# Shorter fill matmuls, a last product in two parts, and another planned order in a one-core attention and mixer kernel on Trainium2

## The chip, the cores and the metric

The kernel runs on one core of a Trainium2 chip. The core has a matmul engine (TensorE, PE in the profile, with its weight loads as PEld), three engines for elementwise work and copies (VectorE or DVE, ScalarE or ACT, GpSimd or POOL), SyncE (SP), which here only issues transfers, and 16 DMA engines fed by queues. Each engine works through its own instructions in the order in which the program gives them and waits at semaphores for the others. PE multiplies a stationary operand (at most 128 x 128, loaded into the array) by a moving one and adds into banks of PSUM, each 128 partitions x 512 f32. The metric is the time of one execution on the device in microseconds (us), lower is better; the median of several runs is given.

## The reference

Attention over a window of 128 keys with a linear bias by distance, 8 batches, 8 heads, 576 positions, 64 numbers per head, and then a mixer: a hidden layer over the tokens and one over the channels, each with a residual. Inputs and outputs are f32.

```python
scores = q @ k.transpose(0, 1, 3, 2) / 8.0
bias = slopes[h] * -abs(i - j);  mask = (i - j >= 0) & (i - j < 128)
attn = softmax(where(mask, scores + bias, -1e9))
x = (attn @ v).transpose(0, 2, 1, 3).reshape(8, 576, 512)
h = relu(x.transpose(0, 2, 1) @ w_tok1) @ w_tok2      # w_tok1 576x256, w_tok2 256x576
u = x + h.transpose(0, 2, 1)
out = u + relu(u @ w_ch1) @ w_ch2                     # w_ch1 512x1536, w_ch2 1536x512
```

## The kernel before

All matmuls are in bf16. A batch of 576 positions is four blocks of 128 and a tail of 64; two batches form a pair, and the two tails of a pair share one block of 128. For every batch there are two strands of work. The `side` strand brings the attention and the token half: loads of q, k, v by POOL with a cast to bf16 on the way (`load`, L515), transposes of q and k, on PE for the first ten blocks (L630, copied out on L636) and by DMA from SP for later ones (L619), scores (L670, with the bias on L679), exp on ACT (L693), the mask on DVE (L703), the product with v (L736), reciprocal and normalising on DVE (L749, L752), then the two token products (L781 and L791; relu on L799 or L800; L820 and L824) and the sum u in `ub` (L842). u is transposed to `uT` by DMA (L850, four transfers a batch) or by PE (L859, L865). The `main` strand is the channel half: the first product in chunks of four matmuls with 512 columns (`chunk`, L1021; L1006 in the head of the kernel), relu on ACT or DVE (L1027, L1028), sums of the hidden blocks (L1046), the tail's share (L1064, L1069, L1109, L1116, stored on L1126), and `second`: the second product, 512 x 1536 by 1536 x 512, as seven products of half size in the manner of Strassen (`PRODUCTS`, numbered 1 to 7). Each product is twelve matmuls of 256 columns (L1198, two groups of six) into a bank, where later products add to what is there. When a product is done, DVE adds it to u or to an output tile `ob` (`evict`, L1169), and the last addition to a tile is followed by a store of 256 KB (L1181), by SP, or by POOL in batches 5 and 6. In the last batch, part of the first channel product is done by seven products too (`unit`, L943, with keeps on L958 and L959 and joins on L967).

The weight pieces of w_ch1 (`A0` to `A3`) and w_ch2 (`B0` to `B3`) and those of the token layer come in on POOL's queue among the loads of the first pair, in the order of the string `LOADS`: `k7` is the k of the seventh block, and so on. POOL issues them one after another, each as soon as its buffer is free.

The order of the whole work is not that of the program text. Each operation is entered into `Plan` with an engine, a modelled cost, a rank, and the buffers that it makes and uses. `Plan.run` (from L118) replays the kernel by its costs: at each step the engine that can start first takes the ready operation of the lowest rank; the rank is the place of the operation in its strand, shifted by a random number of up to 1500 either way (`SEEDS`, one seed per part; part 0 is the first `side`, part b + 1 holds `main` of batch b and `side` of batch b + 1; a seed of 0 means no shift). `emit` (L301) then writes the instructions in the order of the replayed times. What stands where, on every engine, therefore hangs on the modelled costs and on the seeds; the chip keeps to this order on each engine and takes its own times.

Where the replay sees PE wait in the first 60 us, `emit` puts matmuls on a tile of zeros into a bank that is free then (`spin`, L1250, the matmul on L1254), so that PE doesn't stand still. A fill is made for each wait over 60 ns (250 after 20 us). Its length in columns is the wait, plus 150 ns, times 1.2 for waits before 7.4 us; after that it is the wait times 2.4, less 60 ns if it lies after 20 us. There are 43 such matmuls, of 19196 columns together.

At the end of the kernel, the last batch's products come in the order 1, 5, 6, 2, 3, 7, 4. Between products 7 and 4, nine matmuls of the tail (L1109) have their place. The last three transfers are a store of product 7's tile, two small ones of the tail (64 KB each) and then the 256 KB store behind product 4.

Of the kernel before, what the change touches and what calls it, by code (L numbers as in the profile page):

```python
# [11 lines left out]
ALU = mybir.AluOpType  # L12
# [53 lines left out]
class Plan:  # L66
# [51 lines left out]
    def run(self):  # L118
# [87 lines left out]
        while todo:  # L206
            best = None
            for e, c in cand.items():
                pick, early = None, None
                for o in c:  # L210
                    if e == "POOL" and o is not pool[sent]:
                        continue
                    t = max(ready[o], free[e])
# [46 lines left out]
            if e == "PE":  # L260
                slow = 2.0 if t < WARM else 1.0
                if t > free[e] + 1.0:
                    self.gaps.append((free[e], t))
                    if t > free[e] + 3000:
                        slow = 1.6
                    t += 60.0
                elif o.mode != mode:
                    t += 95.0
                mode = o.mode
                o.t0 = t  # L270
                free[e] = t + o.cost * slow
                o.done = free[e] + 165.0
            elif e == "ACT":
                o.t0, free[e], o.done = t, t + o.cost - 115, t + o.cost
            elif e == "DVE":
                o.t0, free[e], o.done = t, t + max(o.cost - 80, 50), t + o.cost
            elif e == "SP":
                o.t0 = t
                if o.bus:
                    free[e] = t + 1310.0  # L280
                    if o.bus > 1500 and len(turns) > 1:
                        free[e] = max(free[e], turns[-2].done + 1100)
                    turns.append(o)
                    send(o, t + 300, 1, TURN[o.bus > 1500][0], TURN[o.bus > 1500][1])
                else:
                    free[e] = t + 590
                    send(o, t + 300, 1, STORE, 1010.0)
            else:
                o.t0 = t
                free[e] = t + o.cost  # L290
                send(o, t + o.cost, 0, STORE if o.packets < 0 else o.packets * PACKET, 1010.0 if o.packets < 0 else LATE[t > FETCH])
                lanes.append(o)
                sent += 1
# [7 lines left out]
    def emit(self, spin):  # L301
        banks = self.rings["ps"]
        fills = []
        for a, z in self.gaps:
            if a < FILL and z - a > (250 if a > DENSE else 60):
                for i, log in enumerate(banks.log):
                    spans = [(min(u.t0 for u in b.users), max(u.done for u in b.users)) for b in log]
                    if all(z1 < a - 50 or a1 >= z for a1, z1 in spans):
                        fills.append((a, i, (z - a + MORE) * 1.2 if a < CHILLY else (z - a - (60 if a > DENSE else 0)) * 2.4))
                        break  # L310
        work = [(o.t0, o.n, o.emit) for o in self.ops]
        work += [(a, -1, lambda i=i, n=n: spin(banks.slots[i], n)) for a, i, n in fills]
        for _, _, go in sorted(work, key=lambda w: w[:2]):
            go()
# [19 lines left out]
RANKH = 0  # L334
RELU = 350
SUMS_AT = 60e3
SEEDS = [45795, 495947, 190309, 331881, 0, 67117, 67408, 179769, 445757]
SHIFT = 1500.0
UNIT_LATE = False
SECOND_LATE = True  # L340
# [8 lines left out]
FILL = 60000.0  # L349
DENSE = 20000.0  # L350
CHILLY = 7400.0
MORE = 150.0
START = 2700.0
PACKET = 0.813
LATE = (2400.0, 2790.0)
# [5 lines left out]
EARLY = 1  # L361


LOADS = ("k3 q3 q2 k2 k1 q1 v0 W2 k8 q8 v2 v1 v3 v8 W1 q7 k7 A0 k5 q5 k4 v5 "
         "q4 A1 v4 k6 q6 A2 v7 v6 A3 T0 B0 B1 B2 B3")


# [1 line left out]
def kernel(  # L369
# [50 lines left out]
    def bank(choice=ONE):  # L420
        return plan.buf("ps", choice)
# [289 lines left out]
    def values(pr, blk, half, pb, rank):  # L711
# [12 lines left out]
        for es in ([[0, 1]] if both else [[0], [1]]):  # L724
# [7 lines left out]
            for at, e in enumerate(es):  # L732
                def go(e=e, at=at, view=view):
                    mms = [(a, z, kind, vb, i, h) for a, z, kind, vb in work for i, h in enumerate(HEADS[e])]
                    for m, (a, z, kind, vb, i, h) in enumerate(mms):
                        pe_.matmul(view()[a:z, at, i, :], lhsT=pb()[:, e, i, kind, a:z], rhs=vb()[:, h, 0 : D + 1],  # L736
                                   start=m == 0, stop=m == len(mms) - 1, skip_group_check=True)

                rk = rank(240)
                plan.op("PE", 120 * len(work) + (110 if tail and half is None else 0), go, rk,  # L740
                        mode=2 if half is not None else 0, reads=[(pb, e)], uses=[w[3] for w in work],
                        **({"adds": ot} if at else {"makes": ot}))

# [391 lines left out]
    def second(b, rank, r2, ss, sums, ub):  # L1135
        pr, half = b // 2, b % 2
        g1, g2, g3 = bank(ANY), bank(ANY), bank(ANY)
        obs = {}
        capt = {}

        def s_of(i):
            return lambda t, c: ss()[:, "124".index(i), t, c * P : (c + 1) * P]
# [44 lines left out]
                plan.op("SP", 550, store, rk, uses=[ob])  # L1187

        DONE = {1: (0, 0, False), 5: (1, 1, False), 6: (0, 1, False), 7: (1, 1, True), 2: (0, 0, True), 3: (0, 1, True), 4: (1, 0, True)}
        for m in PRODUCTS:  # L1190
            l, w, s, tt = L[m]
            bk = BANK[m]
            for g in range(2):
# [18 lines left out]
                if m in AFTER:  # L1212
                    needs.append(capt[AFTER[m]])
                op = plan.op("PE", 656, go, rank(656), reads=rd, needs=needs,
                             **({"makes": bk} if g == 0 and m not in AFTER else {"adds": bk}))
                if SECOND_LATE and g == 0 and m not in AFTER:
                    marks["wait"].append(op)
            evict(m, bk, *DONE[m])

    def along(base, length, total):  # L1220
        done = [0.0]
# [68 lines left out]
```

## Time and profile before

| what | value |
| --- | --- |
| median of 3 runs | 279.54 us (279.27 to 280.08) |
| the profiled execution | 280.54 us |
| its span in the profile | 278.6 us |
| mean granted clock of TensorE | 0.997 |
| PE busy | 271.4 us, 97% of the span |
| DVE, ACT, POOL busy | 208.0, 136.0, 116.0 us |
| moved by DMA | 38.43 MB, mean 138 GB/s |

The span is the time between the first and the last record of the profile; the execution's own time is 1.94 us longer. Times in views count from the start of the span. Matmuls are pipelined: the duration of a record (379 ns for 512 columns) is longer than its distance to the next one, so PE's busy time joins overlapping records, and a short wait can be hidden in it. The waits view has one row for each pair of a waiting line and what it waited for, with the sum in us, the number of waits and the longest. The chain of work is followed back from the last instruction, and its pieces are given with start, length and line. A view by stretches gives the length of each stretch and then, engine by engine, its busy time and the number of instructions.

### The profile page before, as it was taken

The numbers are of one execution on the slowest core, as the hardware profiler recorded it, in microseconds if no ns is written. First come the engines' busy times: TensorE is split into PE (matmuls) and PEld (weight loads), VectorE is DVE, ScalarE is ACT, GpSimd is POOL, SyncE is SP. The second block draws the span as 40 slices with busy tenths as digits, with TensorE's granted clock in tenths as the row PEclk, the third lists the DMA queues.
The fourth block names the chain that finished last, engine by engine and source line by source line (L and its number), as shares of the span: only waits on it lengthen the run. The fifth ranks groups of instructions, "written<-read, shape, count | busy, mean of one in ns | idle before, by whom it ended". The sixth has DMA issues, their size and how long they took to land.

```text
span 278.6 us, 6964 instructions
## 1 busy us (share of the span) xinstructions
PE 271.4 (97%) x2825; PEld 180.0 (65%) x2825; DVE 208.0 (75%) x485; ACT 136.0 (49%) x219; POOL 116.0 (42%) x146
## 2 busy tenths in 40 slices
PE   7999999999999999999999999999999999999994
PEld 3664765675686556585567655486667645689883
DVE  7566689978897559862989479673989549876982
ACT  5561885336960189206961097206870079205610
POOL 8999765940256027900486009700472220013000
PEclk9999999999999999999999999999999999999998
DMA  9999999999899999999999979999499750043014
GB/s 133 155 138 152 182 190 192 155 125 203 141 113 100 172 251 123 123 142 180 182 133 158 205 191 88 148 138 240 69 115 99 197 142 2 2 118 129 0 53 137
DMA packets 167535, 38.43 MB, mean 138 GB/s; under 512 B 155792, under 2 KB 166672, under 8 KB 167504
## 3 DMA queue, kind: packets, MB, share of 16 engines
q0 software_dynamic: 116112, 20.03, 92.8%
q1 hardware_dynamic: 50352, 17.70, 32.9%
q8 instruction: 22, 0.36, 0.6%
q10 hardware_dynamic: 1040, 0.26, 0.4%
q14 instruction: 9, 0.07, 0.1%
HBM read 35.85 MB, written 9.44 MB: 163 GB/s over the span
## 4 chain that ended last, share of the span: by engine, by line
PE 85%; DMA 6%; POOL 3%; DVE 2%; issue 1%; ACT 1%; SPq 0%; POOLq 0%
PE ps L1198 25%; PE ps L1021 25%; PE ps L736 6%; PE ps L670 5%; PE ps L824 5%; PE ps L781 5%; PE ps L1064 4%; PE ps L943 3%; PE ps L1109 3%; POOL qk L515 3%; DMA qk<-in_k_dram 2%; DMA qk<-in_q_dram 2%; DMA uT<-ub 1%; PE ps L630 1%; PE ps L791 1%
## 5 line engine op out<-in xcount | busy, mean ns | idle before, releaser
L1021 PE MATMUL ps<-uT,WC 128*128 128x512 bf16 x328 | 79.3, 379 | 0.8 <-DMA uT<-ub 0.7
L693 ACT ACTIVATE pe<-ps 128x1024 bf16<-128x1024 f32 (+1 forms) x76 | 63.4, 888 | 30.4 <-PE ps L670 30.1
L515 POOL DMA_DIRECT2D v<-in_v_dram x40 | 34.0, 860 | 92.8 <-PE ps L736 89.0
L1027 ACT ACTIVATE r<-ps 128x512 bf16<-128x512 f32 x75 | 44.4, 601 | 41.4 <-PE ps L1021 39.6
L1021 PEld LDWEIGHTS <-WC 128*128 128x128 bf16 x328 | 29.1, 98 | 31.1 <-issue 2.3
L703 DVE TENSOR_TENSOR pe<-pe,mask 128x1024 bf16<-128x1024 bf16 (+1 forms) x64 | 38.1, 608 | 9.0 <-ACT pe L693 8.5
L1198 PEld LDWEIGHTS <-r 128*128 128x128 bf16 x384 | 37.1, 98 | 7.3 <-issue 0.2
L515 POOL DMA_DIRECT2D qk<-in_k_dram x39 | 33.8, 873 | 2.9 <-DMA v<-in_v_dram 1.4
L515 POOL DMA_DIRECT2D qk<-in_q_dram x39 | 33.5, 864 | 2.4 <-DMA WC<-in_moe_w_ch_dram 1.3
L1198 PEld LDWEIGHTS <-s 128*128 128x128 bf16 x288 | 27.5, 98 | 5.9 <-issue 1.3
L752 DVE TENSOR_TENSOR xb<-ps,rt 128x256 bf16<-128x256 f32 (+1 forms) x72 | 29.0, 416 | 0.7
L736 PEld LDWEIGHTS <-pe 128*128 128x128 bf16 (+1 forms) x560 | 22.4, 100 | 9.2 <-DVE pe L703 2.1
L736 PE MATMUL ps<-v,pe 128*128 128x65 bf16 (+1 forms) x560 | 26.5, 194 | 0.1
L1198 PE MATMUL ps<-WC,r 128*128 128x256 bf16 x192 | 25.4, 273 | 0.0
L1198 PE MATMUL ps<-WT,s 128*128 128x256 bf16 x192 | 24.6, 273 | 0.0
L1198 PE MATMUL ps<-WT,r 128*128 128x256 bf16 x192 | 23.9, 273 | 0.0
L1169 DVE TENSOR_TENSOR ob<-ps,ub 128x512 f32<-128x512 f32 x22 | 15.0, 685 | 10.3 <-PE ps L1198 10.1
L842 DVE TENSOR_TENSOR ub<-ps,xb 128x512 bf16<-128x512 f32 x34 | 21.2, 681 | 1.9 <-PE ps L824 1.8
L670 PEld LDWEIGHTS <-qkT 64*128 64x128 bf16 x560 | 14.8, 94 | 11.2 <-issue 9.8
L670 PE MATMUL ps<-qkT 64*128 64x128 bf16 (+1 forms) x304 | 19.4, 216 | 0.0
L749 DVE RECIPROCAL rt<-ps 128x4 f32<-128x4 f32 (+1 forms) x76 | 12.4, 175 | 8.8 <-PE ps L736 8.2
L1069 ACT ACTIVATE r2t<-ps 128x512 bf16<-128x512 f32 x12 | 7.2, 602 | 22.5 <-PE ps L1064 22.5
(95 smaller groups left out, 340.1 us busy)
## 6 DMA issues: line engine op xcount, KB each, us to landing
out_dram<-ob SPq DMA_DIRECT2D x17, 256.0 KB, 2.6
v<-in_v_dram POOLq DMA_DIRECT2D x32, 128.0 KB, 5.3
qk<-in_k_dram POOLq DMA_DIRECT2D x31, 128.0 KB, 5.5
qk<-in_q_dram POOLq DMA_DIRECT2D x31, 128.0 KB, 5.0
WC<-in_moe_w_ch_dram POOLq DMA_DIRECT2D x8, 384.0 KB, 9.1
out_dram<-raw SPq DMA_DIRECT2D x7, 256.0 KB, 2.8
out_dram<-ob POOLq DMA_DIRECT2D x5, 256.0 KB, 3.4
out_dram<-raw POOLq DMA_DIRECT2D x3, 256.0 KB, 2.9
```

The lines of the kernel that those rows point to most:

```text
L515: nc.gpsimd.dma_start(out=to()[p0 : p0 + n, :, :], in_=rows(src, b, s0, n))
L670: pe_.matmul(wide(e)[:, i, kind, a:z], lhsT=ts[kb]()[e * D : (e + 1) * D, NHP + i, :], rhs=ts[blk]()[e * D : (e + 1) * D, i, a:z], start=n ...
L693: act_.activation(out=pb()[:, e, :, lo:, c0:c1_], in_=wide(e)[:, :, lo:, c0:c1_], func=ACT.Exp, scale=scale)
L703: dve_.tensor_tensor(out=o, in0=o, in1=heads(mk, es), op=ALU.mult)
L736: pe_.matmul(view()[a:z, at, i, :], lhsT=pb()[:, e, i, kind, a:z], rhs=vb()[:, h, 0 : D + 1], start=m == 0, stop=m == len(mms) - 1, skip_g ...
L752: dve_.tensor_tensor(out=x4(), in0=view()[r0:r1_, :, :, 0:D], in1=rt()[r0:r1_, 0:n, :, :].broadcast_to([r1_ - r0, n, 4, D]), op=ALU.mult)
L781: pe_.matmul(t1[j]()[:, :], lhsT=W1[:, c, j * P : (j + 1) * P], rhs=xb()[:, blk, :], start=c == 0, stop=False)
L842: plan.op("DVE", 690, lambda blk=blk, ht=ht, hs=hs: dve_.tensor_tensor(out=ub()[:, blk, :], in0=ht()[:, hs], in1=xb()[:, blk, :], op=ALU.a ...
L1021: pe_.matmul(ct()[:, :], lhsT=WC1[:, cb, t * P : (t + 1) * P], rhs=uT()[:, cb, :], start=cb == 0, stop=cb == NCB - 1)
L1027: plan.op("ACT", 600, lambda t=t, ct=ct: act_.activation(out=r2()[:, t, :], in_=ct()[:, :], func=ACT.Relu), rk, part=(r2, t), uses=[ct], o ...
L1169: dve_.tensor_tensor(out=v, in0=bk().rearrange("p (c n) -> p c n", c=2), in1=src, op=ALU.add)
L1198: pe_.matmul(bk()[:, c * HN : (c + 1) * HN], lhsT=l(t, c), rhs=w(t), start=first, stop=g == 1 and t == HK - 1, skip_group_check=True)
```

## The change

1. Fills: a wait is filled if it is over 60 ns before 7.4 us, over 170 ns from there to 20 us and over 250 ns after that; the 150 ns are no longer added, and after 7.4 us the fill is shorter by 120 ns. There are 37 matmuls of 16296 columns.
2. Loads: `k2` and `q2` swap places, and so the order `q7 k7 A0 k5 q5 k4` becomes `q7 q5 k7 A0 k5 k4`.
3. Planner: a store's modelled transfer goes by its cost (half for a half store), a matmul of the product with v is put at 123 ns instead of 120, and five seeds are others. From the second batch on the order of operations is a different one; the operations are the same.
4. The last batch: product 2 moves to the end, in two parts (`last_product`). Each part is six matmuls into a bank of its own, an addition on DVE of 128 x 256 with what product 1 left in `ob`, and a store of 128 KB, the first by SP and the second by ACT. The first part stands behind product 7 and the second behind product 4. The nine matmuls of the tail that stood between 7 and 4 come earlier.

In the instructions as they are written out, the matmuls apart from the fills and last_product are the same in number and shape, and so are the changes from one kind of matmul to another. In the head, the fill of two matmuls that stood between the transposes of q7, k7 and the six of L824 now stands ahead of the transposes (two of 348 columns).

```diff
-                    send(o, t + 300, 1, STORE, 1010.0)
+                    send(o, t + 300, 1, STORE * o.cost / 550, 1010.0)
...
-            if a < FILL and z - a > (250 if a > DENSE else 60):
+            if a < FILL and z - a > (250 if a > DENSE else 60 if a < CHILLY else 170):
...
-                        fills.append((a, i, (z - a + MORE) * 1.2 if a < CHILLY else (z - a - (60 if a > DENSE else 0)) * 2.4))
+                        fills.append((a, i, (z - a) * 1.2 if a < CHILLY else (z - a - 120) * 2.4))
...
-SEEDS = [45795, 495947, 190309, 331881, 0, 67117, 67408, 179769, 445757]
+SEEDS = [45795, 495947, 190309, 317838, 0, 119438, 0, 583887, 0]
...
-LOADS = ("k3 q3 q2 k2 k1 q1 v0 W2 k8 q8 v2 v1 v3 v8 W1 q7 k7 A0 k5 q5 k4 v5 "
+LOADS = ("k3 q3 k2 q2 k1 q1 v0 W2 k8 q8 v2 v1 v3 v8 W1 q7 q5 k7 A0 k5 k4 v5 "
...
-                plan.op("PE", 120 * len(work) + (110 if tail and half is None else 0), go, rk,
+                plan.op("PE", 123 * len(work) + (110 if tail and half is None else 0), go, rk,
...
-        for m in PRODUCTS:
+        for m in PRODUCTS if b < B - 1 else [x for x in PRODUCTS if x != 2] + [2]:
+            if b == B - 1 and m == 2:
+                last_product(b, rank, r2, obs[0, 0], [opened[7], op])
+                continue
...
+    def last_product(b, rank, r2, old, last):
+        for c in range(2):
+            bk, ob = bank(ANY), plan.buf("ob")
+            def go(c=c, bk=bk):
+                for t in range(HK):
+                    pe_.matmul(bk()[:, 0:HN], lhsT=r2()[:, HK + t, c * P : (c + 1) * P], rhs=WC2[:, HK + t, 0:HN],
+                               start=t == 0, stop=t == HK - 1)
+            def add(c=c, bk=bk, ob=ob):
+                dve_.tensor_tensor(out=ob()[:, 0:HN], in0=bk()[:, 0:HN], in1=old()[:, c * HN : (c + 1) * HN], op=ALU.add)
+            def store(c=c, ob=ob):
+                (nc.sync, nc.scalar)[c].dma_start(out=out[b, c * P : (c + 1) * P, 0:HN], in_=ob()[:, 0:HN])
+            rk = rank(656)
+            plan.op("PE", 656, go, rk, reads=[(r2, HK + t) for t in range(HK)], needs=lc2[HK : 2 * HK], makes=bk,
+                    behind=last[c : c + 1])
+            plan.op("DVE", 425, add, rk, makes=ob, uses=[bk, old])
+            plan.op("SP", 275, store, rk, uses=[ob])
```

More of the change, by code (lines that the diff above doesn't have):

```diff
@@ L351 @@
 CHILLY = 7400.0
-MORE = 150.0
 START = 2700.0
@@ L1138, in second @@
         obs = {}
-        capt = {}
+        capt, opened = {}, {}
         def s_of(i):
```

1 line of the change is left out of this document (added).

## The prediction

> **What bounds the kernel now.** I read the page's first three sections, then TensorE's own waits, then its busy time by stretch, and only then the places where a wait stands.
>
> ```profile
> PE 271.4 (97%) x2825; PEld 180.0 (65%) x2825; DVE 208.0 (75%) x485; ACT 136.0 (49%) x219; POOL 116.0 (42%) x146
> ...
> PEclk9999999999999999999999999999999999999998
> ...
> PE 85%; DMA 6%; POOL 3%; DVE 2%; issue 1%; ACT 1%; SPq 0%; POOLq 0%
> ```
>
> TensorE is busy in 97% of the span, at the full granted clock, and holds 85% of the chain that ends last. The next two views say where the other 3% is: its waits, and its busy time in stretches of the span (length, then busy time of PE with its instructions).
>
> ```profile
> PE ps L1254 <- DVE zero L479: 1.0, 1, 1.0
> PE ps L630 <- DMA qk<-in_q_dram: 0.7, 2, 0.4
> PE ps L1021 <- DMA uT<-ub: 0.7, 1, 0.7
> PE ps L630 <- DVE qk L529: 0.3, 1, 0.3
> PE ps L630 <- DMA qk<-in_k_dram: 0.3, 1, 0.3
> ```
>
> ```profile
> 0.00:37.00 37.00, 34.47 (x408) 20.77 (x409) 24.51 (x77) 21.98 (x38) 32.83 (x45) 1.00 1.80 153
> 37.00:85.00 48.00, 47.89 (x538) 32.15 (x536) 43.78 (x109) 28.20 (x46) 24.28 (x30) 1.00 1.65 155
> 85.00:97.00 12.00, 11.34 (x84) 7.31 (x83) 7.13 (x12) 1.68 (x3) 3.43 (x4) 1.00 1.75 150
> 97.00:223.00 126.00, 125.97 (x1296) 81.08 (x1294) 91.86 (x206) 61.37 (x93) 50.81 (x62) 1.00 1.37 155
> ```
>
> Before 37 us PE idles 2.53 us, and the fills of L1254 hide more waiting there. From 37 to 223 us it idles 0.11 + 0.66 + 0.03 = 0.80 us, and 0.66 of that is the one wait for uT. So the kernel is a stream of matmuls with a load-paced head and a tail after the last matmul. A change of order alone can gain the idle time and what pipelining hides, no more; it can lose without such a bound. One place where a wait is hidden, from the chain and from PE's timeline:
>
> ```profile
> 35.96 0.86 PE ps L1021 x4
> 36.83 1.04 PE ps L1021 x4
> ```
>
> ```profile
> 221.79 0.81 PE L1109 MATMUL ps<-WC,r2t 128*128 128x512 bf16 x3
> 222.61 0.59 PE L1021 MATMUL ps<-uT,WC 128*128 128x512 bf16 x2
> ```
>
> Four matmuls of 512 columns step by 0.86 / 4 = 0.216 us; the next four took 1.04, so 0.18 was waiting for a weight load. Three take 0.65, and the L1021 behind them came 0.82 after their start: 0.17 of waiting (or turning to other operands). What order can win past the head is thus about 0.80 + 0.18 + 0.17 = 1.2 us, and a little more where other waits hide like this.
>
> **The change part by part.** The matmuls are the same set in both orders, except fills (43 of 19196 columns become 37 of 16296) and twelve of L1198 that become last_product. The turns between kinds of matmul are equal in number. So the sum holds only head, waits and tail.
>
> *Shorter fills.* 2900 columns fewer, at 0.216 / 512 us each, are 1.2 us of PE at full rate. Nearly all of it stood where PE waited for loads, so it becomes idle time: 0. The cover is the loads that L630 waits for (PE's second and fifth wait above) up to 36.8 us. Where a fill was longer than its wait it did cost, and the loads edit meets that place:
>
> ```profile
> 24.67 0.40 PE L630 MATMUL ps<-ident,qk 128*128 128x128 bf16 x4 [0.25 <-DMA qk<-in_k_dram]
> 24.90 0.50 PE L1254 MATMUL ps<-zero 128*128 128x400 bf16 x2
> 25.24 0.59 PE L824 MATMUL ps<-r,W 128*128 128x512 bf16 x2
> ```
>
> ```profile
> 18.73 5.89 DMA qk<-in_k_dram
> ```
>
> ```profile
> 18.73 0.90 POOL L515 DMA_DIRECT2D qk<-in_k_dram  x1 [0.40 <-PE ps L736]
> 19.62 0.76 POOL L519 DMA_DIRECT2D WC<-in_moe_w_ch_dram  x1
> 20.36 0.91 POOL L515 DMA_DIRECT2D qk<-in_k_dram  x1
> 21.24 0.90 POOL L515 DMA_DIRECT2D qk<-in_q_dram  x1
> ```
>
> k7 is issued at 18.73, lands 5.89 later at 24.62, and PE goes on at 24.67. Four transposes end at 24.90, and the fill puts L824 off to 25.24. The new order moves this fill ahead of the transposes, so L824 follows them at once: −0.34 if k7 lands when it did.
>
> *New order of loads.* "k2 q2" swaps two loads of one size that the same transposes need, so the later of the two lands as before: 0. "q7 q5 k7" moves k7 behind q5 on POOL. The issues above lie 0.87 to 0.9 apart, and loads land at that pace, so k7 lands at 24.62 + 0.87 = 25.5 if the queue is as full as it was. At best it needs from its own issue at 19.63 only what q7 needed from its issue, 4.56:
>
> ```profile
> 17.41 0.93 POOL L515 DMA_DIRECT2D qk<-in_q_dram  x1 [0.16 <-issue]
> ...
> DMA to landing us min/median/max: 4.6/4.6/4.6
> ```
>
> which gives 24.2 (the second line is the load's line within 17.4 to 18.3 us). Then L824 starts between 24.9 and 26.0 (landing, 0.05 until PE, 0.23 of four transposes, up to 0.2 if the turn isn't covered) against 25.24: −0.3 to +0.75. A gain ends at the next load that PE waits for, at the latest at 36.83. A loss shrinks by the 0.17 of waiting there, to +0.58. Ends: 0 and +0.58. The middle of the landings, 24.85, gives L824 at 25.1 to 25.3, so I take **0**. k7's place in L630 holds PE's queue: L824 and all behind it need nothing from k7, and wait all the same.
>
> *Another order from the second batch on* (seeds, costs of stores and of the values product). PE's work is the same; the question is only which waits come and go. The transposes for the 96 us wait have the same matmuls around them in both orders, so 0.66 stays. At 222 us the last L824 of that batch stands about 10.4 us ahead of the L1021 that needs uT, not 7.2, so up to 0.17 goes (cover counted in matmuls of the order, each at its start-to-start time). Around 206 us two L736 and a chunk of L1021 have no margin left by my count: +0.1 each at most. Other hidden waits of that size may come or go. Sum: −0.35 to +0.5; I take **−0.1**.
>
> *The last product in two parts.* The end of the chain and the timeline of the end:
>
> ```profile
> 272.26 1.15 PE L1109 MATMUL ps<-WC,r2t 128*128 128x256 bf16 x9
> ...
> 272.47 0.69 DVE L1169 TENSOR_TENSOR ob<-ps,ob 128x512 f32<-128x512 f32 x1 [0.62 <-PE ps L1198]
> ...
> 273.25 1.47 PE L1198 MATMUL ps<-WT,r 128*128 128x256 bf16 x12
> 273.45 0.42 DVE L1116 TENSOR_TENSOR raw<-ps,ub 128x256 f32<-128x256 f32 x1 [0.29 <-PE ps L1109]
> ...
> 274.76 0.69 DVE L1169 TENSOR_TENSOR ob<-ps,ub 128x512 f32<-128x512 f32 x1 [0.89 <-PE ps L1198]
> 275.48 0.38 SPq L1181 DMA_DIRECT2D out_dram<-ob  x1
> ```
>
> Count from P, the start of the first matmul behind product 7 (272.26). Before: nine L1109 cover product 7's eviction (done at P + 0.90, L1198 goes on at P + 0.99), twelve matmuls of 0.109 take 1.31, the eviction starts 0.2 later at P + 2.50, lasts 0.69, and the store goes out at P + 3.22. After: only six matmuls of part 0, 0.65, stand there; product 4 waits until P + 0.96 for that eviction, a new stall of 0.3. It ends at P + 2.27, part 1 at P + 2.93. But DVE is then busy with product 4's eviction from P + 2.48 to 3.17, so the last add (128x256: 0.42) runs to P + 3.6, and its store goes at P + 3.65. P itself comes 3 x 0.109 = 0.33 earlier, since 24 matmuls, not 21, lie behind product 7. So the last store goes out 3.65 − 0.33 − 3.22 = 0.10 later, and it is half as large. The landing times of L1126's 64 KB stores and of L1181's 256 KB stores in the tail are these:
>
> ```profile
> DMA to landing us min/median/max: 1.9/2.0/2.0
> ```
>
> ```profile
> DMA to landing us min/median/max: 2.2/2.2/2.2
> ```
>
> 0.2 for 192 KB makes about 0.13 for the 128 KB saved. The Trainium skill (DMA: Bandwidth & Descriptors, "Anatomy of one DMA — SWDGE (gpsimd) path") gives a fixed 2.0 us and bytes by 436 GB/s; by that the halved store would save 0.30, an estimate, and the tail would be 0.2 better. These rows say less; they decide. The store is issued by ScalarE's queue, which no tail row shows: 0 to +0.1. Sum of the tail: −0.05 to +0.15; I take **0**.
>
> **Sum.** Head 0, order −0.1, tail 0. The profiled execution took 280.54, its span 278.6 and 1.94 around it, and becomes 280.4. It lies 1.0 above the median 279.54, of which I forecast the change: **279.4 us**.
>
> **The rivals.** *Slower: transposes of u come late again.* The landings of L850's transposes of uT in 85 to 97 us, then in 212 to 223 us:
>
> ```profile
> DMA to landing us min/median/max: 4.0/5.3/6.8
> ```
>
> ```profile
> DMA to landing us min/median/max: 2.3/2.7/3.5
> ```
>
> Beside loads and other transposes they take 4.0 and more, elsewhere 2.3 to 3.5. If the new order sets one of the later groups beside such traffic, the last lands 4.0 − 2.7 = 1.3 later, and with 0.1 of cover PE's L1021 waits 1.2: 279.4 + 1.2 = 280.6. It decides where a group's cover falls under its landing by more than 0.9. For it: several SP stores swap places with transposes. Against it: the counted cover grew at 222 us and is unchanged at 96.
>
> *Late k7*: PE's L630 holds the queue until 25.5, +0.37 to +0.58: 279.8 to 280.0. For it: the loads' pace; against: the slack that POOL's 0.40 wait shows. With the late transposes it makes 281.1.
>
> *Faster: the waits vanish.* If fewer loads run beside the transposes at 96 us and the last lands 3.3 after its issue instead of 4.0, the 0.66 goes too; with 0.35 of hidden ones: 279.54 − 1.0 = 278.5. Against it: the unchanged order around it.
>
> *The split pays nothing*: its part of the sum is 0 already; if ScalarE issues late, +0.1, inside the forecast.
>
> *The clock.* The fills' row and its window show PE at half rate at the start (460 columns in 3.08 / 8 = 0.385 us against 0.19):
>
> ```profile
> 1.00 3.08 PE L1254 MATMUL ps<-zero 128*128 128x460 bf16 x8 [1.00 <-DVE zero L479]
> ```
>
> If shorter fills left PE at half rate, the head's matmuls after 16 us would cost double: about 1.5 us over a spell of 3, 280.9. Against it: the holes left are 0.3 us at most, and PEclk is full with the 1.00 us hole at the start. The Trainium skill (TensorE: Matmul & The Clock Gate, "Part 1: The HAM clock gate") lets the clock fall only after an idle window of about 3.4 us; by that rule it stays.
>
> **How the numbers follow.** Forecast 0.50, its own range 278.8 to 280.2; late k7 alone 0.13; late transposes, with or without k7, 0.19; waits vanish 0.16; the clock 0.02. Runs of this kernel differ by 0.3%, 0.84 us, so that is the bound of no change: faster under 278.70, slower over 280.38. Faster: 0.16 and 0.04 of the forecast's lower end, 0.20. Slower: 0.19 + 0.02, 0.05 of late k7 with other small waits and 0.04 of the forecast's upper end, 0.30. Same: 0.50. The range leaves out 281 and more (half of the transposes' case) and below 278.4: 278.4 to 280.9.
>
> **What the changed profile would show.** L630's wait for in_k_dram near 24 to 25.5 and L824 against 25.24 decide the head; PE's wait for WC at 36.8 says whether a loss was absorbed. A PE wait for uT near 96 of 0.7 and none larger elsewhere is the forecast; one over 1 us is the slower case. In the tail: twelve L1198 0.3 late behind the eviction of product 7, and a last add of 0.42 straight behind a 0.69 eviction. Wrong would be a PE idle sum from 37 to 272 us under 0.3 or over 1.6, or a PEclk below 9 ahead of the last slice.

## The result, and the profile after

The changed kernel takes 280.82 us (median of 22 runs, 279.80 to 282.08), the kernel before on the same chips 279.84 (22 runs, 279.05 to 281.14): a ratio of 1.0039, 95% interval 1.0027 to 1.0051. It is 1.0 us **slower** by the medians (0.93 by the means), where 279.4 and "no change" were forecast. The number is inside the range of 278.4 to 280.9, the direction is not the one forecast.

The profiled execution of after took 280.65, with a span of 278.5 and so 2.15 around it (before: 280.54, 278.6 and 1.94). The spans of the two profiles are alike, and the medians are not: before's profile lies 0.7 above its median, after's 0.2 under. The runs of before beside which the experiments below were timed have a mean span of 277.8 with a scatter (standard deviation) of 0.5, those of after 278.7 with 0.6. So one profile against another can't show where 1 us went; stretches of it, compared over several profiles, can.

From after's page and its view of TensorE's waits:

```profile
PE 268.9 (97%) x2783; PEld 180.1 (65%) x2819; DVE 207.6 (75%) x483; ACT 137.2 (49%) x219; POOL 115.9 (42%) x146
...
PEclk9999999999999999999999999999999999999998
```

```profile
PE ps L735 <- DMA v<-in_v_dram: 1.1, 1, 1.1
PE ps L1279 <- DVE zero L478: 1.0, 1, 1.0
PE ps L629 <- DMA qk<-in_k_dram: 0.4, 1, 0.4
PE ps L823 <- issue: 0.2, 1, 0.2
```

PE's 2.5 us less of busy time is no gain: 36 matmul records are missing from this trace beside the six fills that are really gone. The clock is full, so the clock rival is out for this run. The wait for uT at 96 us, 0.66 in before, is not in the list, and neither is a larger one; the wait for a v at 12 us is new, and lies in the head.

The middle: from the L1021 behind the wait for uT at 96 us to the first matmul behind product 7, which the prediction quotes for before at 272.26. PE's timeline of before, then of after:

```profile
95.19 0.40 PE L670 MATMUL ps<-qkT 64*128 64x128 bf16 x8
96.25 0.59 PE L1021 MATMUL ps<-uT,WC 128*128 128x512 bf16 x2 [0.66 <-DMA uT<-ub]
```

```profile
95.29 0.40 PE L669 MATMUL ps<-qkT 64*128 64x128 bf16 x8
95.79 1.02 PE L1020 MATMUL ps<-uT,WC 128*128 128x512 bf16 x4
```

```profile
271.53 0.82 PE L1230 MATMUL ps<-WC,r 128*128 128x256 bf16 x6
271.73 0.69 DVE L1168 TENSOR_TENSOR ob<-ps,ob 128x512 f32<-128x512 f32 x1 [0.62 <-PE ps L1200]
...
272.48 1.47 PE L1200 MATMUL ps<-WT,r 128*128 128x256 bf16 x12
...
273.78 0.82 PE L1230 MATMUL ps<-WC,r 128*128 128x256 bf16 x6
273.98 0.69 DVE L1168 TENSOR_TENSOR ob<-ps,ub 128x512 f32<-128x512 f32 x1 [1.17 <-PE ps L1200]
274.64 0.42 DVE L1234 TENSOR_TENSOR ob<-ps,raw 128x256 f32<-128x256 f32 x1
274.70 0.37 SPq L1180 DMA_DIRECT2D out_dram<-ob  x1
275.42 0.36 ACTq L1237 DMA_DIRECT2D out_dram<-ob  x1
```

From 96.25 to 272.26 are 176.01 us in before, 175.68 without the three matmuls that after has behind that point; after needs 271.53 − 95.79 = 175.74. In this pair of profiles the other order of the middle is worth nothing, within 0.1.

The tail does what was worked out, up to the last line. The point P is 271.53; L1200 goes on at P + 0.95 behind the eviction (forecast 0.96), part 1 starts at P + 2.25 (2.27), and the last addition ends at 275.06, P + 3.53 (3.6). But its store goes out on ScalarE only at 275.42, **0.36 after the addition's end**, where SP in before took 0.03 (274.76 + 0.69, then 275.48). The landing of L1237's last store is this:

```profile
DMA to landing us min/median/max: 2.2/2.2/2.2
```

Half as large as before's last store, it lands no sooner (2.2).

### The profile page after: what moved, and what is told of

It reads as the page before. It is cut to its first block, busy times and chain, and to the rows that moved or that the text cites. A ratio compares the mean times of both kernels' runs of the same rounds, so it can differ in the third digit from the quotient of the medians.

```text
span 278.5 us, 6935 instructions
## 1 busy us (share of the span) xinstructions
PE 268.9 (97%) x2783; PEld 180.1 (65%) x2819; DVE 207.6 (75%) x483; ACT 137.2 (49%) x219; POOL 115.9 (42%) x146
## 4 chain that ended last, share of the span: by engine, by line
PE 81%; DMA 4%; DVE 4%; POOL 4%; ACT 3%; issue 2%; POOLq 0%; ACTq 0%
PE ps L1200 26%; PE ps L1020 22%; PE ps L823 5%; PE ps L735 5%; PE ps L669 5%; PE ps L1063 4%; PE ps L780 4%; PE ps L1108 4%; PE ps L942 3%; POOL qk L514 2%; DMA W<-in_moe_w_tok_dram 2%; DMA qk<-in_k_dram 2%; ACT pe L692 2%; ACT r L1026 1%; DVE xb L751 1%
## 5 line engine op out<-in xcount | busy, mean ns | idle before, releaser
L1020 PE MATMUL ps<-uT,WC 128*128 128x512 bf16 x306 | 76.8, 379 | 1.0
L1026 ACT ACTIVATE r<-ps 128x512 bf16<-128x512 f32 x79 | 46.2, 602 | 50.3 <-PE ps L1020 49.0
L1200 PEld LDWEIGHTS <-r 128*128 128x128 bf16 x372 | 35.6, 98 | 6.9 <-issue 1.0
L1200 PEld LDWEIGHTS <-s 128*128 128x128 bf16 x288 | 27.7, 98 | 5.5 <-issue 0.7
L751 DVE TENSOR_TENSOR xb<-ps,rt 128x256 bf16<-128x256 f32 (+1 forms) x73 | 29.6, 417 | 1.0
L1200 PE MATMUL ps<-WT,s 128*128 128x256 bf16 x192 | 24.1, 273 | 0.0
L1200 PE MATMUL ps<-WT,r 128*128 128x256 bf16 x192 | 23.7, 273 | 0.1
L1200 PE MATMUL ps<-WC,r 128*128 128x256 bf16 x180 | 23.6, 273 | 0.0
L1168 DVE TENSOR_TENSOR ob<-ps,ub 128x512 f32<-128x512 f32 x21 | 14.2, 684 | 9.4 <-PE ps L1200 9.4
```

Of the source, the lines that this page charges most:

```text
L751: dve_.tensor_tensor(out=x4(), in0=view()[r0:r1_, :, :, 0:D], in1=rt()[r0:r1_, 0:n, :, :].broadcast_to([r1_ - r0, n, 4, D]), op=ALU.mult)
L1020: pe_.matmul(ct()[:, :], lhsT=WC1[:, cb, t * P : (t + 1) * P], rhs=uT()[:, cb, :], start=cb == 0, stop=cb == NCB - 1)
L1026: plan.op("ACT", 600, lambda t=t, ct=ct: act_.activation(out=r2()[:, t, :], in_=ct()[:, :], func=ACT.Relu), rk, part=(r2, t), uses=[ct], o ...
L1168: dve_.tensor_tensor(out=v, in0=bk().rearrange("p (c n) -> p c n", c=2), in1=src, op=ALU.add)
L1200: pe_.matmul(bk()[:, c * HN : (c + 1) * HN], lhsT=l(t, c), rhs=w(t), start=first, stop=g == 1 and t == HK - 1, skip_group_check=True)
```

## The experiments

Each kernel was timed beside the kernel before on the same chip, whose medians were 279.80, 279.82, 279.81, 279.62 and 279.87 in the five sets; ratios and intervals are against it. Three figures are read from each: the mean time; the mean time outside the span; and, from the profile, the **rest**, the time from the fourth chunk of four or more L1021 (at about 39.6 us) to the span's end, less any wait for uT at 96 us. For before the rest is 278.6 − 39.57 − 0.66 = 238.4; for after it is 278.5 − 39.72 = 238.8. In what follows theory A puts the loss on the tail, B on the middle's order, C on the head (C1 its loads, C2 its fills).

### The tail alone, and after without it

before_newtail adds last_product, the half store's cost and the last seed to before. after_oldtail takes last_product out of after, which doesn't give the old tail back, since the seed is the new one.

```diff
-        for m in PRODUCTS:
+        for m in PRODUCTS if b < B - 1 else [x for x in PRODUCTS if x != 2] + [2]:
...
-SEEDS = [45795, 495947, 190309, 331881, 0, 67117, 67408, 179769, 445757]
+SEEDS = [45795, 495947, 190309, 331881, 0, 67117, 67408, 179769, 0]
```

> The kernel before with the new tail alone (last_product, the seed of the last part, the planner's cost of half stores; head and middle untouched). Theory A, the tail carries the loss: the last store is issued by ScalarE 0.3 late and lands no sooner for being half as large, and PE stands 0.3 between products 7 and 4, so 0.4 to 0.6 us slower than before, with 0.2 of it outside the profile's span. Theory B, the middle's order carries it and the tail is worth nothing as forecast: 0 to 0.1 from before. Theory C, the head (k7 late) carries it: the same as B here.

> The changed kernel with the old tail (products in the old order, no last_product); head and middle are those of after. Against before on the same chip: theory A: +0.4 to +0.6 is left of the change's +1.0, that is 0.4 to 0.6 faster than after. Theories B and C: still +0.9 to +1.0.

before_newtail: 279.58 (12 runs), ratio 0.9994, interval 0.9976 to 1.0011; span 277.7 and 1.95 outside. The split itself costs nothing that shows, and A in this plain form falls. But it isn't quite the tail of after either: two tail pieces of L1126 go out behind ScalarE's store (at 274.95 and 275.48, the store at 274.67), and land last. after_oldtail: 281.56 (7 runs), 1.0061, interval 1.0036 to 1.0086, slower still. Its profile has the wait for uT (0.65) and tail pieces of L1125 as its last stores, landing at 278.70: another tail, not the old one, so it tells nothing on A.

### Both stores by SP

after_sp is after with one edit.

```diff
-                (nc.sync, nc.scalar)[c].dma_start(out=out[b, c * P : (c + 1) * P, 0:HN], in_=ob()[:, 0:HN])
+                nc.sync.dma_start(out=out[b, c * P : (c + 1) * P, 0:HN], in_=ob()[:, 0:HN])
```

> The changed kernel with both stores of last_product issued by SP. Theory A: the last store goes out 0.03 after its addition instead of 0.36, so 0.3 faster than after (+0.7 against before), and if the 0.2 outside the span belongs to ScalarE's issue, 0.5 faster (+0.5). Theories B and C: no more than 0.1 from after (+0.9 to +1.0).

280.29 (12 runs), ratio 1.0026, interval 1.0008 to 1.0043: faster than after by 0.5 in the medians and by 0.3 in the means against before, with intervals that overlap. The last lines of its tail:

```profile
274.94 0.42 DVE L1234 TENSOR_TENSOR ob<-ps,raw 128x256 f32<-128x256 f32 x1
275.01 0.37 SPq L1180 DMA_DIRECT2D out_dram<-ob  x1
275.47 0.42 SPq L1237 DMA_DIRECT2D out_dram<-ob  x1
```

The store follows the addition's end (275.36) by 0.11, and the rest is 238.2. Outside the span it is still 2.14. So a part of the loss seems to hang on who issues the last store. That alone doesn't explain before_newtail, where ScalarE issues too, and 0.08 after its addition's end.

### The head: fills and loads

before_newhead has new fills and new loads, before_newfills and before_newloads one of them each; after_oldhead, after_oldloads and after_oldfills put them back in after. The edits are the lines of the diff on `LOADS`, and on the fills.

```diff
-LOADS = ("k3 q3 q2 k2 k1 q1 v0 W2 k8 q8 v2 v1 v3 v8 W1 q7 k7 A0 k5 q5 k4 v5 "
+LOADS = ("k3 q3 k2 q2 k1 q1 v0 W2 k8 q8 v2 v1 v3 v8 W1 q7 q5 k7 A0 k5 k4 v5 "
...
-            if a < FILL and z - a > (250 if a > DENSE else 60):
+            if a < FILL and z - a > (250 if a > DENSE else 60 if a < CHILLY else 170):
```

> The kernel before with the new fills and the new order of loads; the order from the second batch on and the tail are those of before. Theory C: k7 lands at 25.1 or later, L824 starts 0.2 to 0.6 later than in before and PE keeps that past 36.8 us, so +0.3 to +0.6. Theories A and B: +0.1 to +0.2, the head's share that the two profiles show at 36 us.

> The kernel before with the shorter fills alone; the order of everything else, loads included, is word for word that of before. Theory C1, the new order of loads makes the head late: 0 to 0.1 from before. Theory C2, the shorter fills do it (PE starts late out of an idle spell, or code for PE comes at a worse time): +0.5 to +0.7, as the new head as a whole.

> The kernel before with the new order of loads alone (fills are those that the old rule gives for it). Theory C1: +0.5 to +0.7, with k7 landing at 24.5 or later and L824 behind it. Theory C2: 0 to 0.1.

> The changed kernel with the old fills and the old order of loads; middle and tail are those of after. Theory C (the head carries most): +0.3 against before, what tail and middle are worth in the spans so far, so 0.6 to 0.7 faster than after. Theory A (the tail carries it): still +0.8 to +1.0.

> The changed kernel with the old order of loads and the new, shorter fills. Theory C1 (loads): 0.5 to 0.7 faster than after, +0.3 to +0.5 against before. Theory C2 (fills): as after, +0.9 to +1.1.

> The changed kernel with the old, longer fills and the new order of loads. Theory C1 (loads): as after, +0.9 to +1.1 against before. Theory C2 (fills): 0.5 to 0.7 faster than after, +0.3 to +0.5. If each edit does half, both this and the one with old loads lie at +0.6 to +0.8.

| kernel | loads, fills | median (runs) | ratio, 95% interval | mean span | outside |
| --- | --- | --- | --- | --- | --- |
| before_newhead | new, new | 280.94 (6) | 1.0047, 1.0029 to 1.0064 | 278.4 | 2.49 |
| before_newloads | new, old | 280.28 (12) | 1.0020, 1.0004 to 1.0037 | 278.2 | 2.31 |
| before_newfills | old, new | 280.37 (12) | 1.0018, 0.9995 to 1.0040 | 278.6 | 1.98 |
| after_oldfills | new, old | 281.09 (12) | 1.0042, 1.0022 to 1.0061 | 278.9 | 2.15 |
| after_oldloads | old, new | 279.83 (12) | 1.0001, 0.9987 to 1.0014 | 278.0 | 1.95 |
| after_oldhead | old, old | 279.99 (12) | 1.0009, 0.9994 to 1.0025 | 278.1 | 1.99 |

In the changed kernel the answer is clear: with the old loads it is as fast as before, whatever the fills; with the new loads it is 1 us slower, whatever the fills. C1 holds there, C2 does not, but for before_newfills, which was run again (below). before_newhead is a warning: with nothing of the new tail it is as slow as after. By the means it lies 1.2 above before, 0.7 in the span and 0.5 outside it, and in its profile the rest is 238.2, no more than before's, so that nothing of this shows behind the fourth chunk. A loss of 1 us can thus come without ScalarE's store.

How do loads do it? Not through k7. In after, k7 lands at 25.14 and L823 starts at 25.43, 0.19 later than in before; the rows are these:

```profile
25.19 0.40 PE L629 MATMUL ps<-ident,qk 128*128 128x128 bf16 x4 [0.41 <-DMA qk<-in_k_dram]
25.43 0.38 PE L823 MATMUL ps<-r,W 128*128 128x512 bf16 x1
```

k7 does land later with the new loads: at 23.4 to 25.4 in the profiles with all of them, at 22.3 to 24.6 in those with the old ones. But PE meets the load stream again at the weight piece A2, and there it forgets what came before. From the chain of before_newhead:

```profile
27.71 8.67 DMA WC<-in_moe_w_ch_dram
36.39 0.05 issue
36.43 1.04 PE ps L1021 x4
```

A2 is issued at 27.71, lands 8.67 later at 36.38, and L1021 goes on at once. The fourth chunk starts 2.78 to 2.80 after A2's landing in 18 of the 20 profiles of this study (exceptions: 2.95 in before_newloads, 3.65 in before_nofills). A2 itself lands anywhere between 35.9 and 37.6, with old loads and new: before 36.78, after 36.93, before_newhead 36.39, before_newmiddle 37.57. So what the head costs is A2's landing, and a load 0.2 late at 25 us isn't in it. Nor do the profiles show A2 late for the new loads: it lands at 36.8 in the mean of the seven profiles with all new loads, and at 36.7 in that of the eleven with the old ones (before_nofills and before_q5first left out).

### ScalarE's program

What then differs with the new loads? The planner puts one copy of the transposed u (L865 in before) on ScalarE instead of DVE, so ScalarE's program is one operation and one wait longer. In after and after_oldfills, with the new loads, ScalarE issues its last store 0.36 after the addition's end; in after_oldhead and after_oldloads, with the old ones, 0.08. From after_oldloads:

```profile
274.48 0.42 DVE L1234 TENSOR_TENSOR ob<-ps,raw 128x256 f32<-128x256 f32 x1
...
274.98 0.36 ACTq L1237 DMA_DIRECT2D out_dram<-ob  x1
```

Three kernels separate the program's length from the loads. They add tiny operations on ScalarE at the start: two in after_oldloads_pad2 and before_pad2, eight in after_pad8. Everything else stands as it was.

```diff
+    for _ in range(2):
+        act_.activation(out=masks[0:1, 0, 0, 0, 0:1], in_=dist[0:1, 0, 0:1], func=ACT.Exp, scale=-1.0)
     for e in range(2):
         for i, h in enumerate(HEADS[e]):
             act_.activation(out=masks[:, e, i, :, :], in_=dist[:, :, :], func=ACT.Exp, scale=-float(slopes[h]))
```

> The changed kernel with the old order of loads, and two tiny operations more on ScalarE at the very start (an exp of one number that a later operation writes over), so that its program is as long as with the new order, which puts one copy more on ScalarE. Theory P (the length of ScalarE's program matters at its end): the last store goes out 0.3 after its addition's end instead of 0.03, it lands in 2.2 instead of 2.0, and 2.15 instead of 1.95 lies outside the span: 0.5 to 0.7 slower than with the old order alone, +0.7 against before. Theory L (the loads themselves): as with the old order alone, +0.1 against before.

> The changed kernel with eight tiny operations more on ScalarE at the start. Theory P: its end lies elsewhere in what is fetched at a time, so the lag of the last store can go back to 0.03 and the time outside the span to 1.95: 0.5 to 0.7 faster than after; if the 0.3 stay, the place of the end is not the cause. Theory L: as after, +0.9 to +1.2 against before.

> The kernel before with the same two tiny operations on ScalarE at the start; it has no store on ScalarE at its end. Theory P: the time outside the span grows from 2.0 to 2.3 or 2.5, as with the new loads or the new head, the span stays: +0.3 to +0.5. Theory L: 0.

Old loads with two operations more, then the new loads with eight more:

```profile
274.38 0.42 DVE L1236 TENSOR_TENSOR ob<-ps,raw 128x256 f32<-128x256 f32 x1
...
275.16 0.36 ACTq L1239 DMA_DIRECT2D out_dram<-ob  x1
```

```profile
274.42 0.42 DVE L1236 TENSOR_TENSOR ob<-ps,raw 128x256 f32<-128x256 f32 x1
...
274.92 0.36 ACTq L1239 DMA_DIRECT2D out_dram<-ob  x1
```

The additions end at 274.80 and 274.84, and the stores go out 0.36 and 0.08 later. The lag comes with two operations too many and the old loads, and goes with eight and the new ones. So the lag goes with the length of ScalarE's program, as theory P has it, and not with the loads. It comes with a slower landing as well: 2.2 to 2.3 after the late issue, 2.0 after the early one. The rest is 238.8 in after, after_oldfills and after_oldloads_pad2, the three with the lag; in after_sp, after_oldhead and after_pad8 it is 238.2 to 238.3, as in the kernels with before's middle and tail (238.1 to 238.4). after_oldloads has 238.7 without the lag, of which 0.4 is a wait for uTt that only its profile shows. So lag and landing make **0.5 us** in the profiles.

The traces hold one more hint. The page of after counts ten instruction fetches on queue q14, that of before nine. The last of the ten lies between 276 and 277 us in after, behind the last store's issue; in after_pad8, where only ScalarE's program was made longer, it lies between 259 and 261 us. That speaks for its being ScalarE's, with a border of what it fetches near its program's end. But in after_oldloads, which has no lag, it lies behind the store too (between 276 and 277.5 us), so why two instructions make a lag isn't shown.

In times: after_oldloads_pad2 280.36 (12 runs), 1.0024, interval 1.0009 to 1.0039, against 1.0001 without the two: it moved by all that the rows give (0.5 by the means, 0.7 by the medians). after_pad8 took 280.13, 1.0034, interval 1.0018 to 1.0050, and here the expectation of P failed: its mean span is 278.35 against 278.7 of after, but its mean time lies 0.86 above before on its chip, where after's lies 0.93 above. That is near what theory L forecast, and can't be told from after.

All the kernels with after's tail together, as means against before: with the lag +0.7 (old loads) and +0.9 and +1.2 (new loads); without it +0.1 and +0.2 (old loads), +0.6 (after_sp) and +0.9 (after_pad8). So the lag is worth 0.5 with the old loads and 0.3 with the new ones, each with a standard error of 0.2, and the new loads cost about 0.5 beside it, of which 0.2 lies outside the span.

The time outside the span does not obey P: 1.93 in after_oldloads_pad2, 2.15 in after_pad8, 2.13 in before_pad2 (279.65, 1.0002, interval 0.9986 to 1.0019). It is steady to 0.05 in after's 22 runs, but not in every build: in before_newloads it has two levels, 1.95 to 2.02 in three runs and 2.31 to 2.51 in nine, and before_q5first is alike. Its cause stays open.

### Middle, fills again, and half of the loads

before_newmiddle has the new seeds of parts 3, 5, 6, 7 and 123 ns; before_q5first only the later half of the loads' edit; before_newfills_again is before_newfills once more.

```diff
-SEEDS = [45795, 495947, 190309, 331881, 0, 67117, 67408, 179769, 445757]
+SEEDS = [45795, 495947, 190309, 317838, 0, 119438, 0, 583887, 445757]
...
-LOADS = ("k3 q3 q2 k2 k1 q1 v0 W2 k8 q8 v2 v1 v3 v8 W1 q7 k7 A0 k5 q5 k4 v5 "
+LOADS = ("k3 q3 q2 k2 k1 q1 v0 W2 k8 q8 v2 v1 v3 v8 W1 q7 q5 k7 A0 k5 k4 v5 "
```

> The kernel before with the new seeds of parts 3, 5, 6 and 7 and 123 ns for the product with v; fills by the old rule, loads and tail as before. Theory C: 0 to 0.2 from before, and no wait of PE between 97 and 272 us that before doesn't have. Theory B (the order of the middle carries it): +0.5 to +1.0.

> The kernel before with the shorter fills alone, once more. The first time its mean lay 0.7 above before, with the widest spread of all; within the changed kernel the same fills made no difference. Theory C2 (shorter fills cost time): +0.5 to +0.7 again. Theory C1: -0.2 to +0.2.

> The kernel before with the later half of the new order of loads alone (q7 q5 k7 A0 k5 k4); against the kernel with all new loads it differs in k2 and q2 only. If q5 ahead of k7 is what costs: +0.3 to +0.6 against before. If the swap of k2 and q2 is what costs: 0 to +0.1.

before_newmiddle: 280.43 (12 runs), 1.0021, interval 1.0008 to 1.0034. That is what theory B forecast, but no wait of its middle is new, and its rest is 238.6, 0.2 above before's; its last stores are tail pieces, and land at 277.95. That is a tail that after doesn't have, since last_product changes it again. What the rest of its loss is, the profile doesn't show. The fills again: 280.33 (12), 1.0013, interval 0.9992 to 1.0033. By the means that is +0.7 the first time and +0.3 now, each with a standard error of 0.2 to 0.3, against −0.1 in the mean spans of the two pairs in after: not settled. before_q5first: 279.96 (12), 1.0007, interval 0.9991 to 1.0023, mean span 277.6, and 2.34 outside. before_newloads, which differs from it by "k2 q2" alone, has 278.2. What the new loads cost in the span thus points to the swap of k2 and q2, by 0.5 with a standard error of 0.2, as the expectation had it for the swap; but the two were timed on two chips, and no row shows how.

### No fills past the start

before_nofills keeps the 12 fills of the first 7.4 us and leaves out 31.

```diff
-FILL = 60000.0
+FILL = 7400.0
```

> The kernel before with fills only in the first 7.4 us (12 of 43 left); all other instructions in the same order. It makes the fills edit larger. Theory C2, idle spells of PE in the head cost time by themselves: more than the shorter fills, +0.8 to +2.0 and a granted clock under 0.99 or matmuls at half rate between 8 and 37 us. Theory C1, the head goes by its loads alone: 0 to +0.1, A2's landing at 36.1 to 37.6 as in the profiles so far, PE idle instead of filled.

283.75 (6 runs), 1.0152, interval 1.0119 to 1.0186. Stretches of before and of before_nofills (length, PE's busy time and so on; the figure ahead of the last two is the granted clock):

```profile
14.00:16.00 2.00, 1.77 (x22) 0.76 (x20) 0.41 (x1) 2.00 (x3) 2.00 (x3) 1.00 2.26 142
16.00:18.00 2.00, 1.80 (x20) 1.24 (x21) 1.85 (x3) 1.02 (x2) 1.75 (x4) 1.00 1.86 130
18.00:20.00 2.00, 2.00 (x65) 1.83 (x62) 1.63 (x10) 0.86 (x2) 1.60 (x3) 1.00 1.46 158
```

```profile
8.00:10.00 2.00, 1.04 (x22) 0.72 (x20) 0.82 (x2) 0.85 (x2) 2.00 (x4) 1.00 2.12 135
10.00:12.00 2.00, 1.39 (x23) 1.04 (x18) 0.68 (x1) 1.82 (x2) 2.00 (x3) 1.00 1.41 150
12.00:14.00 2.00, 1.47 (x29) 0.94 (x25) 1.85 (x7) 1.00 (x2) 2.00 (x4) 1.00 2.24 162
14.00:16.00 2.00, 1.21 (x23) 0.89 (x22) 0.38 (x1) 2.00 (x4) 2.00 (x4) 1.00 2.34 146
16.00:18.00 2.00, 1.08 (x21) 1.11 (x22) 1.90 (x4) 0.89 (x1) 2.00 (x5) 0.56 1.97 140
18.00:20.00 2.00, 2.00 (x45) 1.82 (x43) 1.43 (x7) 0.97 (x2) 2.00 (x4) 0.50 1.59 167
20.00:22.00 2.00, 1.78 (x24) 1.37 (x22) 1.87 (x10) 1.05 (x5) 2.00 (x3) 0.50 1.91 119
22.00:24.00 2.00, 1.78 (x7) 0.75 (x6) 0.70 (x3) 0.00 (x0) 2.00 (x4) 0.73 1.26 167
```

The longest idle spell of PE there is that ahead of L736, in PE's timeline of before_nofills:

```profile
16.92 1.48 PE L736 MATMUL ps<-v,pe 128*128 128x65 bf16 x24 [1.19 <-ACT pe L693]
```

Without fills PE was busy for 5.11 of the 8 us from 8 to 16 us, 64%, with no idle spell over 1.2 us, and the granted clock fell to a half from 16.2 to 23.1 us. In windows of 3.41 us, PE was busy for 2.54 us (from 6.00), 2.64 (from 9.41) and 1.85 (from 12.83): the clock stayed full over the first two, and was a half right behind the third. The shorter fills of the change keep PE busy enough: in 24 runs of the two kernels with only the new fills, one had a mean clock under 0.996 (0.994, with the longest span, 280.1).

But the 4 us by which this kernel is slower are not shown to be the clock's. Neither theory forecast as much. One of the six runs had a mean clock of 1.000 and took 283.66, and the two with the lowest, 0.988, were the fastest (282.97 and 283.18). In the profile A2 lands at 35.86, and the fourth chunk starts 3.65 behind it, 0.9 more than elsewhere, but at 39.51 no later than in before (39.57). Most of what this profile loses comes later: PE waits 1.0 us for uT at 96 us and 2.0 at 225 us, which wasn't followed up.

### Another split

before_split4 leaves before's order and splits product 4's own end: its matmuls go by halves of the bank, each half with its own addition of 128x256 and its own store by SP. It was run twice.

```diff
-                    for c in range(2):
-                        for t in range(3 * g, 3 * g + 3):
+                    for c in [g] if halves_ else range(2):
+                        for t in range(HK) if halves_ else range(3 * g, 3 * g + 3):
...
+                if halves_:
+                    half_out(b, rank, bk, g, ub)
+            if not halves_:
+                evict(m, bk, *DONE[m])
```

> The kernel before with its last product in two parts in another way: product 4 stays last, its twelve matmuls go by halves of the bank, and each half has its own addition (128x256) and its own store by SP; nothing else moves. Both theories: the last addition takes 0.42 instead of 0.69, so the last store goes out 0.27 earlier after the last matmul, it lands as late after its issue as the whole one (2.17), and the execution is 0.2 to 0.3 faster than before, which the medians may not tell from 0; the end of the profile does.

> The kernel before with product 4's addition and store in halves, once more, to see whether it beats before. Both theories: 0.2 to 0.4 faster than before.

279.29 (12 runs), 0.9988, interval 0.9972 to 1.0004; again 279.69 (12), 1.0003, interval 0.9990 to 1.0017. The tail of its profile, and the landing of its two last stores:

```profile
272.61 1.47 PE L1199 MATMUL ps<-WT,r 128*128 128x256 bf16 x12
...
274.12 0.76 DVE L1230 TENSOR_TENSOR ob<-ps,ub 128x256 f32<-128x256 f32 x2 [0.88 <-PE ps L1199]
274.58 0.97 SPq L1233 DMA_DIRECT2D out_dram<-ob  x2
```

```profile
DMA to landing us min/median/max: 1.8/1.8/1.8
```

Here the expectation failed: the first half's addition starts at 274.12, 1.51 after L1199's first matmul, when all twelve are done and not six. So nothing overlaps, the last addition ends at 274.88, 2.27 after that matmul (before: 275.45 − 273.25 = 2.20), and the second store goes out at 275.13, 2.52 after it (before 2.23), behind the first on SP. What is gained is the landing, 1.8 instead of 2.2: the last byte lands 4.3 after that matmul, not 4.4. The rest is 238.0, 0.1 to 0.4 less than in the kernels with before's tail. The profile shows a gain of 0.1 to 0.4; the times don't tell it from none. No version here clearly beats before.

## Why the prediction was wrong

*The step that failed is the end of the tail*: "The store is issued by ScalarE's queue, which no tail row shows: 0 to +0.1", and with it "0.2 for 192 KB makes about 0.13 for the 128 KB saved". The issue came 0.33 later after the addition than SP's, and nothing was saved in landing. Lag and landing make 0.5 in the profiles of six kernels, and 0.3 to 0.5 in the mean times, each with a standard error of 0.2. The bound of 0.1 had no row behind it. The lag goes with the length of ScalarE's program, which wasn't among the rivals. The Trainium skill (DMA: Bandwidth & Descriptors, "Anatomy of one DMA — SWDGE (gpsimd) path") has the figures, for GpSimd's path, by which the halved store would save 0.30, an estimate. In after, where ScalarE issues it, it saves nothing, at 2.2; in before_split4, where the 128 KB store follows another by 0.55 on SP, 1.8 against 2.2 is near it.

*1.94 around the span* was carried over from before. It is 2.17 in after's runs, 2.0 in before's: 0.2 more, shown, cause open.

*New order of loads: 0.* The range's upper end of +0.58 was for a late k7. L823 did start later (+0.19), but A2's landing, 2.8 us ahead of the fourth chunk in 18 of 20 profiles, wipes it out; "late k7" is refuted as a price. Yet kernels with all new loads have a mean span less their rest of 39.9 to 40.2, against about 39.6 for before (277.8 − 238.2, the middle of the rests with before's tail): about 0.3 of the loss lies in the head or in the wait at 96 us, points to "k2 q2", which I put at 0 by the order of two equal loads, and isn't explained. It isn't clean either: before_newfills and its repeat, with the old loads, have 40.5 and 40.0.

So 0.5 (ScalarE's end) + 0.2 (outside the span) + 0.3 (head) comes to the 1.0, within errors of 0.2 on the first and the last. The lag is shown to go with the program's length, its price is less certain; the second is shown only as a figure, the third only as a difference of means.

*Luck*: that 280.82 lies inside the range. Its upper end was set for late transposes and a slow clock, and neither came.

*Right*: shorter fills cost nothing in after (−0.1 in the mean spans of two pairs); the middle is worth 0 (175.74 against 175.68 us); the stall of 0.3 between products 7 and 4 and every time in the tail up to the last addition, within 0.1; no uT wait over 1 us in after. Of the clock rival, that fills hold the clock is right: with 31 of them left out it falls to a half. Its price of 1.5 is not confirmed: the fourth chunk came 0.9 later behind A2, and that kernel's time doesn't follow the clock.

*Wrong on the basis*: I took the 0.66 wait for uT in before's one profile for a fixed part ("so 0.66 stays"). It is absent in 12 of the other 19 profiles, and 0.2 to 0.6 in six of the rest (1.0 in before_nofills). The profile of before was a long execution, and the idle time that order could win, 1.2 us, was that execution's.

## What to carry to other kernels

Where one execution differs from the next by more than the effect sought, cut the profile at a point that resets what came before (here the landing of one weight load) and compare what follows it over several profiles. A last store belongs on the queue that the trace has shown to issue at once; here, moving it to an engine with a program of its own cost more than halving it saved. And an edit far from the end can change the end by making one engine's program two instructions longer, so look at each engine's count, not at PE alone. Last, a fall of the clock in a trace is not yet a cost: look whether the work behind it comes later.

## What the runs showed of the hardware

- ScalarE's last DMA issue came 0.08 or 0.36 after the result that it waited for, by the number of instructions ahead of it: 0.36 with two more, 0.08 with ten more. Which property of the program decides wasn't found.
- The granted clock fell to 0.50 at about 16 us (before_nofills) without any idle spell of PE over 1.2 us, behind 3.41 us in which PE was busy for 1.85; it had stayed full with 2.54 and 2.64. The Trainium skill (TensorE: Matmul & The Clock Gate, "Part 1: The HAM clock gate") names in its table an idle window of about 3.4 us for this, and further down a kernel whose PE idles briefly but often. The trace agrees with the second: many short waits were enough.
- A 128 KB store at the end landed in 1.8 to 2.3 us, a 256 KB one in 2.2 to 2.3: the landing didn't go by the size alone.
- The time outside the profile's span has means of 1.92 to 2.49 us over builds that differ by as little as two instructions or the order of two loads.
